# Loading every sixth K tile of an attention kernel by three transfers, of 112, 8 and 8 partitions

## The chip, the cores and the metric

The kernel runs on one core of a Trainium2 chip. The metric is the device time of one execution in microseconds (us). Kernels that were timed ran in alternating rounds with the kernel before, on the same chip. A run more than 1.5% above the fastest of its kernel is called slow, the others fast. The kernel before takes 861.65 us (median of the first 3 runs, 858.39 to 861.66; with two more it is 859.63 us below). In the profiles PE is TensorE, DVE is VectorE, ACT is ScalarE, POOL is GpSimd and SP is SyncE, which issues the transfers; PEld is the loading of weights into TensorE.

## The reference

Two attention blocks whose outputs are concatenated. Block A has 4 K/V heads for 32 query heads; block B, which the change touches, has 32 K/V heads.

```python
def _B_ref(x, k_cache, v_cache, wq, wo):
    B, Sq, D = x.shape                     # 16, 32, 1024
    H, Dh = 32, 128                        # k_cache, v_cache: (16, 32, 1024, 128) bf16
    q = (x @ wq).reshape(B, Sq, H, Dh).transpose(0, 2, 1, 3)
    scores = jnp.einsum("bhqd,bhkd->bhqk", q, k_cache) * (Dh ** -0.5)
    p = _softmax(scores, axis=-1)
    o = jnp.einsum("bhqk,bhkd->bhqd", p, v_cache)
    return o.transpose(0, 2, 1, 3).reshape(B, Sq, H * Dh) @ wo
```

B alone reads 128 MiB of K and as much of V, once each.

## The kernel before

The kernel lists its operations with their buffers, orders them with a scheduler of its own, and works out the semaphore waits. All transfers are issued from SP. A step of B takes four heads of one batch entry: a K tile of 1 MiB and a V tile of 1 MiB.

```python
KB_sb = sb("KB_sb", [P, NKB, 2, 16 * Dh], BF)      # NKB = 2 K tiles of B, 8192 B per partition each
VB_sb = sb("VB_sb", [P, NVB, 4, NCH, Dh], BF)      # NVB = 3 V tiles of B
# ... cut ...
def st_dmaK(q):
    # ... A's K tile cut ...
    sl = q.krslot
    ksrc = pb["k"][q.b, q.h0:q.h0 + 4].rearrange("a (p s) d -> (a p) (s d)", s=32)
    pr.add("sp", lambda e: e.dma_start(KB_sb[:, sl, :, :].rearrange("p i n -> p (i n)"), ksrc),
           writes=[("KB", sl)], dma_key=f"kb{sl}", name="kb_dma", dur=4 * Sk * Dh * 2, wtag={("KB", sl): q.kid})

def st_dmaV(q):
    # ... A's V tile cut; B's: two transfers of two heads each, pieces of 2048 B
    vsrc = pb["v"][q.b, q.h0 + 2 * t_:q.h0 + 2 * t_ + 2].rearrange("a (p c) d -> p a c d", c=NCH)
    # ...
```

A row of the K tile, one partition's share, is 8192 contiguous bytes. VectorE transposes the tile (two instructions of 1.23 us), which frees the buffer for the next load.

Of the kernel before, what the change touches and what calls it, by code (L numbers as in the profile page):

```python
# [12 lines left out]

RINV_LOW, RINV_HIGH = 1e-10, 1e10
NVB_SLOTS = 3
NKB_SLOTS = 2
LAZY_PER_STEP = 100
LAZY_DELAY = 0
# [40 lines left out]
class Prog:  # L59
# [8 lines left out]
        self.specs = []  # L68
        self.vtag = {}

    def add(self, eng, emit, reads=(), writes=(), dma_key=None, name="", dur=None, tag=None, prio=0, wtag=None, rtag=None):
        if rtag:
            for r_, v_ in rtag.items():
                have = self.vtag.get(r_, None)
                assert have == v_, "version mismatch on %r: op %s expects %r but buffer holds %r" % (r_, name, v_, have)
        if wtag:
            for r_, v_ in wtag.items():
                self.vtag[r_] = v_
        if dur is None:
            dur = DUR.get(name, 0.2)  # L80
        self.specs.append((eng, emit, tuple(reads), tuple(writes), dma_key, name, dur, tag, prio))
        op = _Op(eng, emit, name, dur, tag)
        op.prio = prio
        op.idx = len(self.ops)
        deps = {}
        for r in reads:
            w = self.last_w.get(r)
            if w is not None and w is not op:
                deps[w] = 1
        for w_ in writes:  # L90
            lw = self.last_w.get(w_)
            if lw is not None and lw is not op:
                deps[lw] = 1
            for rd in self.readers.get(w_, ()):
                if rd is not op:
                    deps[rd] = 1
        for r in reads:
            self.readers.setdefault(r, []).append(op)
        for w_ in writes:
            self.last_w[w_] = op  # L100
            self.readers[w_] = []
        op.deps = list(deps.keys())
        if dma_key is not None:
            op.dma_key = dma_key
            self.dma_count[dma_key] = self.dma_count.get(dma_key, 0) + 1
            op.dma_val = 16 * self.dma_count[dma_key]
        self.ops.append(op)
        return op
# [91 lines left out]
    def list_schedule(self, lat=0.2, dma_bw=DMA_BW, dma_lat=1.8, look=0.1):  # L200
        ops = self.ops
        n = len(ops)
        users = [[] for _ in range(n)]
        ndeps = [0] * n
        for op in ops:
            ndeps[op.idx] = len(op.deps)
            for d in op.deps:
                users[d.idx].append(op.idx)

        def odur(op):  # L210
            if op.dma_key is not None:
                return 0.06 + op.dur / dma_bw + dma_lat
            return op.dur
        bl = [0.0] * n
        for i in range(n - 1, -1, -1):
            m = 0.0
            for u in users[i]:
                v = bl[u] + lat
                if v > m:
                    m = v  # L220
            bl[i] = odur(ops[i]) + m + ops[i].prio + PRIO_BONUS.get(ops[i].name.split("@")[0], 0.0)
        ready_t = [0.0] * n
        free = {}
        ready = {}
        for i in range(n):
            if ndeps[i] == 0:
                ready.setdefault(ops[i].eng, []).append(i)
        order = []
        pe_mode = [0]
        sp_order = [i for i in range(n) if ops[i].eng == "sp"]  # L230
        sp_pos = [0]
        dma_free = [0.0]

        def sw(i):
            if ops[i].eng != "pe":
                return 0.0
            return MODE_SWITCH if PE_MODE.get(ops[i].name, 0) != pe_mode[0] else 0.0
        while True:
            best = None
            bkey = None  # L240
            for eng, lst in ready.items():
                if not lst:
                    continue
                fe = free.get(eng, 0.0)
                if eng == "sp":
                    fe = max(fe, dma_free[0] - SP_AHEAD)
                if eng == "sp" and SP_STRICT:
                    ci = sp_order[sp_pos[0]]
                    if ci not in lst:
                        continue  # L250
                    st = max(ready_t[ci], fe)
                    key = (st, -bl[ci])
                    if bkey is None or key < bkey:
                        bkey = key
                        best = ci
                    continue
                emin = min(max(ready_t[i], fe) + sw(i) for i in lst)
                cand = [i for i in lst if max(ready_t[i], fe) + sw(i) <= emin + look]
                ci = max(cand, key=lambda i: (bl[i] - 8.0 * sw(i), -i))
                st = max(ready_t[ci], fe) + sw(ci)  # L260
                key = (st, -bl[ci])
                if bkey is None or key < bkey:
                    bkey = key
                    best = ci
            if best is None:
                break
            op = ops[best]
            ready[op.eng].remove(best)
            if op.eng == "sp":
                sp_pos[0] += 1  # L270
            st = max(ready_t[best], free.get(op.eng, 0.0)) + sw(best)
            if op.eng == "sp":
                st = max(st, dma_free[0] - SP_AHEAD)
            if op.eng == "pe":
                pe_mode[0] = PE_MODE.get(op.name, 0)
            op.t0 = st
            if op.dma_key is not None:
                free[op.eng] = st + 0.06
                xs = max(st + 0.06, dma_free[0])
                dma_free[0] = xs + op.dur / dma_bw  # L280
                op.t1 = dma_free[0] + dma_lat
            else:
                op.t1 = st + op.dur
                free[op.eng] = op.t1
            order.append(best)
            for u in users[best]:
                uo = ops[u]
                same_pe = (op.dma_key is None and op.eng == uo.eng and uo.eng == "pe")
                r = op.t1 + (0.0 if same_pe else lat)
                if uo.dma_key is not None:  # L290
                    r += DMA_MARGIN.get(uo.name, DMA_MARGIN_DEFAULT)
                if r > ready_t[u]:
                    ready_t[u] = r
                ndeps[u] -= 1
                if ndeps[u] == 0:
                    ready.setdefault(uo.eng, []).append(u)
        assert len(order) == n, "cycle in dependency graph?"
        seq = sorted(range(n), key=lambda k: (ops[order[k]].t0, k))
        newp = Prog()
        for k in seq:  # L300
            eng, emit, reads, writes, dma_key, name, dur, tag, prio = self.specs[order[k]]
            newp.add(eng, emit, reads, writes, dma_key, name, dur, tag, prio)
        return newp

    def report(self, a, b, engs=("pe", "act", "dve", "sp")):
# [21 lines left out]
    def run_engine(self, eng_name, eng, sems):  # L327
        for op in self.ops:
            if op.eng != eng_name:
                continue  # L330
            for key, val in op.waits:
                eng.wait_ge(sems[key[1]], val)
            last = op.emit(eng)
            if op.dma_key is not None:
                last.then_inc(sems[op.dma_key], 16)
            elif op.sig is not None:
                last.then_inc(sems[op.eng], 1)

# [143 lines left out]
def build(nc, pa, pb, out):  # L482
    P = 128
# [5 lines left out]
    Dh = pa["k"].shape[3]  # L489
    Sk = pa["k"].shape[2]  # L490
# [26 lines left out]
    pr = Prog()  # L517
    with contextlib.ExitStack() as stack:
# [24 lines left out]
        KB_sb = sb("KB_sb", [P, NKB, 2, 16 * Dh], BF)  # L543
# [231 lines left out]
        def st_dmaK(q):  # L775
            if q.pi == 0:
                if not q.kv_new:
                    return
                sl = q.kvslot
                pr.add("sp", lambda e: e.dma_start(KA_sb[:, sl, :, :], pa["k"][q.b, q.s].rearrange("(p c) d -> p c d", c=NCH)),  # L780
                       writes=[("KA", sl)], dma_key=f"ka{sl}", name="ka_dma", dur=Sk * Dh * 2, wtag={("KA", sl): q.kid})
            else:
                sl = q.krslot
                ksrc = pb["k"][q.b, q.h0:q.h0 + 4].rearrange("a (p s) d -> (a p) (s d)", s=32)
                pr.add("sp", lambda e: e.dma_start(KB_sb[:, sl, :, :].rearrange("p i n -> p (i n)"), ksrc), writes=[("KB", sl)], dma_key=f"kb{sl}", name="kb_dma", dur=4 * Sk * Dh * 2, wtag={("KB", sl): q.kid})

        def st_dmaV(q):
            if q.pi == 0:
# [367 lines left out]
```

## Time and profile before

| | before |
|---|---|
| time | 861.65 us |
| DMA rate over the profiled span | 398 GB/s |
| PE, DVE, ACT busy | 84%, 63%, 52% |
| chain of waits, share of DMA | 53%, of which K tiles of B 40% |
| 8192 B packets: median | 309 ns |

The chain of waits is the work that ended last, followed back from the last instruction. A packet is one piece that a DMA engine moves: for a K tile, one row: the page counts 16507 packets of 8 KB or more (135547 less 119040), 16384 rows of 128 tiles and 123 of instructions.

The page of the kernel before, cut to its lines on DMA: the busy share of the DMA engines in 40 slices of the span (9 is 90% or more), the rate in each slice, the packets and the queue that carries the loads.

```profile
DMA  9999999999999999999999999999999999999994
GB/s 341 366 400 412 413 412 389 413 415 399 413 400 385 413 410 412 402 400 411 403 412 404 406 411 401 411 408 408 413 403 412 412 409 412 414 411 409 411 384 174
DMA packets 135547, 341.57 MB, mean 398 GB/s; under 512 B 10496, under 2 KB 26880, under 8 KB 119040
...
q1 hardware_dynamic: 135424, 339.78, 101.1%
```

The engines are busy from start to end at a rate that hardly varies. The packets are the other half of the reading: the trace records each one, and an 8192 B packet takes 309 ns, 26.5 GB/s on one engine; sixteen such engines give 424 GB/s. So the engines run as fast as their packets let them.

The same kernel in stretches of 8 us, from the table by stage (start and end, length, busy times of the engines with instruction counts, clock, DMA share, GB/s):

```profile
170.00:178.00 8.00, 7.82 (x141) 4.44 (x140) 6.16 (x13) 3.71 (x9) 1.04 (x1) 1.00 1.03 411
178.00:186.00 8.00, 7.60 (x131) 4.21 (x131) 4.74 (x9) 5.42 (x13) 0.24 (x1) 1.00 1.04 412
186.00:194.00 8.00, 6.28 (x106) 4.28 (x107) 4.91 (x12) 5.45 (x12) 0.80 (x1) 1.00 1.03 415
194.00:202.00 8.00, 6.89 (x110) 4.50 (x111) 5.48 (x13) 3.05 (x7) 1.04 (x1) 1.00 1.04 411
```

The last two columns matter: DMA share about 1, rate 411 to 415 GB/s in each of these four.

The longest wait of VectorE (the list of waits: us in total, times, longest), and the transfer of the K tile (count, KB each, median us from issue to landing):

```profile
DVE KBt_sb L820 <- DMA KB_sb<-in_B_k_cache_dram: 93.9, 82, 3.1
```

```profile
KB_sb<-in_B_k_cache_dram SPq DMA_DIRECT2D x128, 1024.0 KB, 9.1
```

### The profile page before, as it was taken

How to read it: one execution, taken by the hardware profiler on the slowest of the kernel's cores; microseconds unless marked ns; L12 is line 12 of the kernel's file. 1: busy time of each engine (PE TensorE's matmuls, PEld its weight loads, DVE VectorE, ACT ScalarE, POOL GpSimd, SP SyncE). 2: the span in 40 equal slices, each digit the busy share in tenths (PEclk: the TensorE clock that was granted, in tenths of full speed). 3: DMA queues.
4: the chain of work that ended last, by engine and by line, in shares of the span. 5: the costliest groups of instructions: out<-in, count | busy, mean ns of one | idle time of the engine just before them, and what ended most of it. 6: DMA issues, size and time to landing. Idle time of an engine off the chain costs nothing.

```text
span 857.6 us, 27298 instructions
## 1 busy us (share of the span) xinstructions
PE 717.3 (84%) x11970; PEld 436.2 (51%) x12098; DVE 541.5 (63%) x1115; ACT 447.1 (52%) x981; POOL 67.9 (8%) x76
## 2 busy tenths in 40 slices
PE   3999998898978789888897979988889778878885
PEld 2546655455545455555554545545455445545452
DVE  1655566666657477577674756757777656666674
ACT  1456766466544464546554545544565554555452
POOL 0001000100000000000000000000000000000000
PEclk9999999999999999999999989999999999999898
DMA  9999999999999999999999999999999999999994
GB/s 341 366 400 412 413 412 389 413 415 399 413 400 385 413 410 412 402 400 411 403 412 404 406 411 401 411 408 408 413 403 412 412 409 412 414 411 409 411 384 174
DMA packets 135547, 341.57 MB, mean 398 GB/s; under 512 B 10496, under 2 KB 26880, under 8 KB 119040
## 3 DMA queue, kind: packets, MB, share of 16 engines
q1 hardware_dynamic: 135424, 339.78, 101.1%
q8 instruction: 96, 1.57, 0.7%
q14 instruction: 27, 0.22, 0.1%
HBM read 337.64 MB, written 2.10 MB: 396 GB/s over the span
## 4 chain that ended last, share of the span: by engine, by line
DMA 53%; PE 19%; DVE 15%; SPq 6%; issue 4%; ACT 2%; POOL 1%; POOLq 0%; DVEq 0%
DMA KB_sb<-in_B_k_cache_dram 40%; DVE KBt_sb L820 12%; DMA VA_sb<-in_A_v_cache_dram 5%; PE ps_pj L709 4%; PE ps_s L855 3%; DMA woA_sb<-in_A_wo_dram 3%; PE ps_pj L651 3%; PE ps_pj L668 2%; SPq L800 2%; PE ps_o L947 2%; PE ps_kt L913 2%; SPq L682 1%; PE ps_s L838 1%; PE ps_pt L897 1%; DMA woB_sb<-in_B_wo_dram 1%
## 5 line engine op out<-in xcount | busy, mean ns | idle before, releaser
L820 DVE STREAM_TRANSPOSE KBt_sb<-KB_sb 128x1024 f32<-128x1024 f32 x256 | 306.1, 1226 | 97.7 <-DMA KB_sb<-in_B_k_cache_dram 93.9
L878 ACT ACTIVATE P_sb<-ps_s 128x512 bf16<-128x512 f32 x256 | 152.4, 600 | 84.1 <-PE ps_s L855 74.5
L870 ACT ACTIVATE PTA_sb<-ps_s 128x1024 bf16<-128x1024 f32 x128 | 131.3, 1026 | 104.2 <-PE ps_s L838 91.5
L855 PE MATMUL ps_s<-KBt_sb,QB_sb 32*32 32x512 bf16 x4096 | 146.9, 395 | 10.1 <-DVE KBt_sb L820 5.5
L582 ACT COPY PT_sb<-ps_pt 128x512 f32<-128x512 f32 x128 | 74.9, 585 | 105.7 <-PE ps_o L947 88.6
L794 POOL COPY VAp_sb<-VA_sb 128x1024 bf16<-128x1024 bf16 x64 | 66.6, 1041 | 761.9 <-DMA VA_sb<-in_A_v_cache_dram 729.4
L897 PE MATMUL ps_pt<-id,P_sb 128*128 128x128 f32 x512 | 105.5, 305 | 9.3 <-ACT P_sb L878 7.3
L947 PE MATMUL ps_o<-VB_sb,PT_sb 128*32 128x128 bf16 x4096 | 81.6, 221 | 23.7 <-DMA VB_sb<-in_B_v_cache_dram 16.6
L897 PEld LDWEIGHTS ps_pt<-id,P_sb 128*128 128x128 f32 x512 | 82.7, 206 | 35.2 <-ACT P_sb L878 17.7
L947 PEld LDWEIGHTS ps_o<-VB_sb,PT_sb 128*32 128x32 bf16 x4096 | 60.0, 97 | 60.2 <-issue 56.9
L913 PE MATMUL ps_kt<-VAp_sb,PTA_sb 128*128 128x129 bf16 x1024 | 80.8, 222 | 10.9 <-POOL VAp_sb L794 4.9
L913 PEld LDWEIGHTS ps_kt<-VAp_sb,PTA_sb 128*128 128x128 bf16 x1024 | 67.5, 99 | 36.5 <-POOL VAp_sb L794 14.9
L838 PE MATMUL ps_s<-QT_sb,KTA_sb 128*128 128x256 bf16 x512 | 82.2, 275 | 3.0 <-DVE KTA_sb L584 2.0
L855 PEld LDWEIGHTS ps_s<-KBt_sb,QB_sb 32*32 32x32 bf16 x4096 | 49.3, 90 | 60.9 <-DVE KBt_sb L820 10.6
L709 PE MATMUL ps_pj<-woA_sb,OTA_sb 128*128 128x512 bf16 x224 | 64.0, 394 | 17.4 <-DMA woA_sb<-in_A_wo_dram 10.0
L963 DVE TENSOR_SCALAR OB_sb<-ps_o,rinv_all 128x128 bf16<-128x128 f32 x128 | 43.7, 342 | 53.4 <-PE ps_o L947 52.6
L709 PE MATMUL ps_pj<-woB_sb,OTB_sb 128*128 128x512 bf16 x206 | 62.0, 394 | 16.6 <-ACT OTB_sb L582 4.5
L668 PE MATMUL ps_pj<-xT_sb,wq_sb 128*128 128x512 bf16 x234 | 64.2, 389 | 8.4 <-DMA wq_sb<-in_B_wq_dram 3.4
L651 PE MATMUL ps_pj<-xT_sb,wq_sb 128*128 128x512 bf16 x232 | 63.9, 380 | 8.3 <-DMA wq_sb<-in_A_wq_dram 4.1
L883 DVE TENSOR_TENSOR stat<-stat 64x1 f32<-64x1 f32 x256 | 41.9, 164 | 32.0 <-ACT P_sb L878 24.4
L838 PEld LDWEIGHTS ps_s<-QT_sb,KTA_sb 128*128 128x128 bf16 x512 | 45.0, 98 | 25.5 <-issue 4.4
L722 DVE TENSOR_TENSOR acc<-acc,ps_pj 128x512 f32<-128x512 f32 x64 | 43.0, 672 | 20.1 <-PE ps_pj L709 19.7
(49 smaller groups left out, 533.0 us busy)
## 6 DMA issues: line engine op xcount, KB each, us to landing
KB_sb<-in_B_k_cache_dram SPq DMA_DIRECT2D x128, 1024.0 KB, 9.1
VB_sb<-in_B_v_cache_dram SPq DMA_DIRECT2D x256, 512.0 KB, 9.8
KA_sb<-in_A_k_cache_dram SPq DMA_DIRECT2D x64, 256.0 KB, 10.3
VA_sb<-in_A_v_cache_dram SPq DMA_DIRECT2D x64, 256.0 KB, 9.6
wq_sb<-in_B_wq_dram SPq DMA_DIRECT2D x32, 256.0 KB, 8.6
wq_sb<-in_A_wq_dram SPq DMA_DIRECT2D x32, 256.0 KB, 8.5
woB_sb<-in_B_wo_dram SPq DMA_DIRECT2D x32, 256.0 KB, 10.8
woA_sb<-in_A_wo_dram SPq DMA_DIRECT2D x32, 256.0 KB, 10.1
```

The costliest lines, as they stand in the source:

```text
L582: pr.add("act", lambda e: e.copy(dst_ap, src_ap), reads=reads, writes=writes, name=name + "@act", wtag=wtag, rtag=rtag)
L651: last = e.matmul(ps_pj[:, 0:tn], wq_sb[:, 0, j, hc * Dh:(hc + 1) * Dh], xT_sb[:, 0, j, t0:t0 + tn], start=(j == 0), stop=(j == DJ - 1))
L668: last = e.matmul(ps_pj[:, 0:NTOK], w, xT_sb[:, 1, j, :], start=(j == 0), stop=(j == DJ - 1))
L709: last = e.matmul(ps_pj[:, 0:OUTW], OT[:, gp, hh, :], wo_[:, hh, oh * OUTW:(oh + 1) * OUTW], start=(hh == 0), stop=(hh == nh - 1))
L820: pr.add("dve", lambda e: e.transpose(KBt_sb[:, sl, t_, :].bitcast(F32).rearrange("p (s r i) -> p s r i", r=2, i=32), KB_sb[:, rs, t_, :]. ...
L838: last = e.matmul(ps_s[:, sbf, c2, i * 2 * P:(i + 1) * 2 * P], KTA_sb[:, sl, c * P:(c + 1) * P], qt, start=True, stop=True)
L855: last = e.matmul(ps_s[32 * cg:32 * cg + 32, sbf, g, :].rearrange("p (sh cl j) -> p sh cl j", sh=4, cl=4), lhsT, kt[32 * a:32 * a + 32, g, ...
L870: pr.add("act", lambda e: e.activation(dst, src, ACTF.Exp, scale=scale), writes=BK_S[sbf] + [("PTA", q.half)], name="expA", rtag={("Sv", s ...
L878: pr.add("act", lambda e, src=src, dst=dst, g=g: e.activation(dst, src, ACTF.Exp, scale=scale, accum_out=st[:, g:g + 1]), writes=[BK_S[sbf ...
L897: last = e.transpose(ps_pt32[:, m * P:(m + 1) * P], p32[:, m:Sk // 2:NPK], id32[:])
L913: last = e.matmul(ps_kt[:, qh * OA0:qh * OA0 + Dh + 1], PTA_sb[:, h, c, qh * P:(qh + 1) * P], VAp_sb[:, sl, 4 * h + c, 0:Dh + 1], start=(h ...
L947: last = e.matmul(ps_o[32 * a:32 * a + 32, 0:Dh], PT_pairs[:, c // 2, 32 * (a ^ (c // 4 * 2)):32 * (a ^ (c // 4 * 2)) + 32, c % 2], VB_sb[ ...
```

## The change

Every sixth K tile of B, 21 of 128, is cut into rows 0 to 111, 112 to 119 and 120 to 127. The intent, as the name in the code (LOW_EVERY) suggests, is to move load onto some of the DMA engines: if a transfer of 8 partitions is spread over 8 engines only, and both small transfers over the same 8, those carry 9 rows of the tile and the others 7. The rest of the diff lets an operation hold several transfers that count on one semaphore.

```diff
+LOW_EVERY = 6
@@ Prog.add, run_engine and the scheduler (cut): an operation has n_dma transfers
-            self.dma_count[dma_key] = self.dma_count.get(dma_key, 0) + 1
+            self.dma_count[dma_key] = self.dma_count.get(dma_key, 0) + n_dma
...
-                last.then_inc(sems[op.dma_key], 16)
+                for one in last if isinstance(last, list) else [last]:
+                    one.then_inc(sems[op.dma_key], 16)
@@ st_dmaK
-                pr.add("sp", lambda e: e.dma_start(KB_sb[:, sl, :, :].rearrange("p i n -> p (i n)"), ksrc), ...
+                kdst = KB_sb[:, sl, :, :].rearrange("p i n -> p (i n)")
+                cuts = [(0, P - 16), (P - 16, P - 8), (P - 8, P)] if q.t % LOW_EVERY == LOW_EVERY - 1 else [(0, P)]
+                pr.add("sp", lambda e: [e.dma_start(kdst[a:b], ksrc[a:b]) for a, b in cuts], ...
```

More of the change, by code (lines that the diff above doesn't have):

```diff
@@ L69, in __init__, with add @@
         self.vtag = {}
-    def add(self, eng, emit, reads=(), writes=(), dma_key=None, name="", dur=None, tag=None, prio=0, wtag=None, rtag=None):
+    def add(self, eng, emit, reads=(), writes=(), dma_key=None, name="", dur=None, tag=None, prio=0, wtag=None, rtag=None, n_dma=1):
         if rtag:
@@ L80, in add @@
             dur = DUR.get(name, 0.2)
-        self.specs.append((eng, emit, tuple(reads), tuple(writes), dma_key, name, dur, tag, prio))
+        self.specs.append((eng, emit, tuple(reads), tuple(writes), dma_key, name, dur, tag, prio, n_dma))
         op = _Op(eng, emit, name, dur, tag)
@@ L300, in list_schedule @@
         for k in seq:
-            eng, emit, reads, writes, dma_key, name, dur, tag, prio = self.specs[order[k]]
-            newp.add(eng, emit, reads, writes, dma_key, name, dur, tag, prio)
+            eng, emit, reads, writes, dma_key, name, dur, tag, prio, n_dma = self.specs[order[k]]
+            newp.add(eng, emit, reads, writes, dma_key, name, dur, tag, prio, n_dma=n_dma)
         return newp
@@ L784, in st_dmaK @@
                 ksrc = pb["k"][q.b, q.h0:q.h0 + 4].rearrange("a (p s) d -> (a p) (s d)", s=32)
-                pr.add("sp", lambda e: e.dma_start(KB_sb[:, sl, :, :].rearrange("p i n -> p (i n)"), ksrc), writes=[("KB", sl)], dma_key=f"kb{sl}", name="kb_dma", dur=4 * Sk * Dh * 2, wtag={("KB", sl): q.kid})
+                kdst = KB_sb[:, sl, :, :].rearrange("p i n -> p (i n)")
+                cuts = [(0, P - 16), (P - 16, P - 8), (P - 8, P)] if q.t % LOW_EVERY == LOW_EVERY - 1 else [(0, P)]
+                pr.add("sp", lambda e: [e.dma_start(kdst[a:b], ksrc[a:b]) for a, b in cuts], writes=[("KB", sl)], dma_key=f"kb{sl}", name="kb_dma",
+                       dur=4 * Sk * Dh * 2, wtag={("KB", sl): q.kid}, n_dma=len(cuts))
         def st_dmaV(q):
```

## The prediction

> **What bounds the kernel.** The DMA engines. The page shows mean DMA busy "9" in 39 of 40 slices, 398 GB/s over the span, and the hardware queue alone takes 101.1% of 16 engines' span; PE is at 84%, DVE 63%, ACT 52%. The chain of waits is 53% DMA, 40% of it the load of the K tile of B. In the trace's packet records an 8192 B packet takes 309 ns and the next one starts about 306 ns after it, so a balanced K tile (8 rows on each of 16 engines) occupies an engine for about 2.45 us. The count of packets in flight is 16 or, beside an instruction fetch, 15 nearly all the time: no engine has slack. The landings of one transfer on its 16 engines are spread over about 2.5 us, over 4 us at the end, where 7 or 8 engines are early and 8 late.
>
> **What the change does.** 21 of the 128 K tiles (every sixth) change. Bytes and schedule stay. 42 more issues of about 0.45 us on SP, some 19 us, are off the critical path: SP issues 656 in 862 us and waits for buffers for most of the rest.
>
> [...]
>
> 1. Load alone:[...] 21 x 0.306 = 6.4 us (0.75%)[...].
> [...]
>
> The base is saturated, so nearly all of either is on the critical path. [...]
>
> **Prediction: 890 us, 858 to 945. Faster by over 2%: 0.02; within 2%: 0.45; slower by over 2%: 0.53.**
>
> **What would show it.** DMA rate falls from 398 GB/s to about 385; median packet of 8 KB stays 309 ns, but some 300 to 2,000 of them take 0.6 to 1.5 us[...]. With load alone: no longer packets[...]. DVE waits for K tiles, 93.9 us now, grow by about what the kernel loses.
>
> [...]

Passages are cut, and marked. The sum itself was this. By the estimate from the trace, a K tile of 128 rows takes an engine 8 x 0.306 = 2.45 us. A changed tile was put at 7 x 0.306 = 2.1 us for the 112 rows and 2 x 1.22 us for the two small transfers, 4.6 us together: 2.1 us more, 21 times, 45 us. The 1.22 us, four times the 0.306 us of the trace, was an assumption. One row more on some of the engines, the 6.4 us, was the smaller alternative; "either" is these two. The 45 us were discounted to 30, hence 890 us. The 309 and 306 ns, the packets in flight and the landings are from the trace of the kernel before, where each of the 656 transfers has 16 landing packets (10496); the 0.45 us of an issue is an estimate from the issues there (medians of 0.34 to 0.47 us for the K and V loads). Cut too: 858 to 868 us if the larger term came to nothing, and over 945 us if the 112 rows cost something themselves.

## The result

| | before | after |
|---|---|---|
| time, median of 5 | 859.63 us (858.39 to 861.66) | 950.69 us (942.17 to 952.69) |
| ratio | | 1.104 (95% interval 1.100 to 1.109) |
| profiled span | 857.6 us | 940.3 us |
| DMA rate | 398 GB/s | 363 GB/s |
| 8192 B packets that took over 386 ns (a quarter above 309) | 242 | 2851 |
| 2048 B packets that took over 105 ns (a quarter above 84) | 484 | 7486 |

A ratio is the mean time of one kernel's fast runs over that of the other's fast runs of the same rounds, so not quite the ratio of the medians quoted. Where a difference in us is given below for a timed run, it is (ratio - 1) times the median before of the same rounds: here 0.104 x 859.6 = 90 us slower.

The page of the kernel after:

```profile
DMA  9999999999999999999999999999999999999994
GB/s 336 375 370 400 331 361 369 350 413 341 393 360 412 351 381 373 360 374 339 378 353 391 364 412 345 336 411 354 407 324 359 408 338 406 330 397 350 390 325 163
DMA packets 135887, 341.61 MB, mean 363 GB/s; under 512 B 10833, under 2 KB 27217, under 8 KB 119377
...
q1 hardware_dynamic: 135760, 339.78, 100.3%
```

The engines are as busy as before (100.3% against 101.1%), with the same bytes, at a lower rate. This is a busy share that hides a slowdown: the packets themselves take longer. Slices near 412 GB/s stand beside slices of 324 to 341.

The packets under 512 B grew from 10496 to 10833. They are taken to be the packets that report the landing of a share: 10496 is 16 for each of the 656 transfers. Then 42 small transfers with 8 shares each make 336 of the 337 more. So each small transfer ran in 8 shares, and the 112-row transfers kept their 16. That 8 shares are 8 of the 16 engines agrees with the DMA share of 0.48 at which 8-row loads alone ran (below).

The stretches around one changed tile, whose three transfers are issued together from 177.35 us (the timeline of SP):

```profile
177.35 1.14 SPq L789 DMA_DIRECT2D KB_sb<-in_B_k_cache_dram  x3
```

```profile
170.00:178.00 8.00, 5.29 (x104) 2.72 (x90) 6.02 (x8) 4.30 (x9) 1.04 (x1) 1.00 1.02 400
178.00:186.00 8.00, 7.83 (x98) 5.10 (x96) 5.25 (x10) 4.58 (x11) 1.04 (x1) 1.00 1.00 259
186.00:194.00 8.00, 5.36 (x90) 3.00 (x87) 4.28 (x10) 3.22 (x7) 0.00 (x0) 1.00 1.03 385
194.00:202.00 8.00, 7.02 (x129) 3.83 (x127) 5.75 (x10) 5.35 (x11) 1.04 (x1) 1.00 1.05 420
```

In the 8 us after the issue the rate is 259 GB/s at a DMA share of 1.00; two stretches later it is back at 420. Each changed tile makes such a burst: by the packet records, each of the 21 is followed within 16 us by a stretch of 8 us at 217 to 320 GB/s. From 412 to 259 GB/s for 8 us is a loss of (412 - 259) x 8 / 412 = 3.0 us, and 1.3 us more are lost on average in its flanks and elsewhere (90 / 21 = 4.3 us per changed tile).

The packet records close the account. Summed over all packets, the time above the medians grew by 707 engine-us for the 8192 B packets, 490 for the 2048 B packets, which the change does not touch, and 19 for the 1024 B ones. That is 1216 / 16 = 76 us per engine, of the 82.7 us by which the profiled spans differ.

```profile
DVE KBt_sb L825 <- DMA KB_sb<-in_B_k_cache_dram: 138.4, 74, 6.4
```

```profile
KB_sb<-in_B_k_cache_dram SPq DMA_DIRECT2D x107, 1024.0 KB, 10.8
KB_sb<-in_B_k_cache_dram SPq DMA_DIRECT2D x21, 896.0 KB
...
KB_sb<-in_B_k_cache_dram SPq DMA_DIRECT2D x42, 64.0 KB
```

VectorE's wait for K tiles grew by 44.5 us only. Other waits on landed data grew too: that of POOL for V tiles of A from 729.4 to 820.2 us, that of PE for V tiles of B from 16.6 to 34.3 us.

### The profile page after: what moved, and what is told of

Same layout as the page of the kernel before. It is cut to its first block, busy times and chain, and to the rows that moved or that the text cites. A ratio compares the mean times of both kernels' runs of the same rounds, so it can differ in the third digit from the quotient of the medians.

```text
span 940.3 us, 27468 instructions
## 1 busy us (share of the span) xinstructions
PE 758.5 (81%) x12098; PEld 447.9 (48%) x12098; DVE 544.2 (58%) x1115; ACT 448.8 (48%) x981; POOL 67.9 (7%) x76
## 3 DMA queue, kind: packets, MB, share of 16 engines
q1 hardware_dynamic: 135760, 339.78, 100.3%
## 4 chain that ended last, share of the span: by engine, by line
DMA 51%; PE 25%; DVE 12%; SPq 6%; issue 3%; ACT 1%; POOL 1%; POOLq 0%; DVEq 0%
DMA KB_sb<-in_B_k_cache_dram 33%; DVE KBt_sb L825 9%; DMA VB_sb<-in_B_v_cache_dram 7%; DMA VA_sb<-in_A_v_cache_dram 6%; PE ps_pj L711 5%; PE ps_s L860 5%; DMA woA_sb<-in_A_wo_dram 3%; PE ps_pj L670 3%; PE ps_o L952 2%; PE ps_pj L653 2%; PE ps_kt L918 2%; PE ps_pt L902 2%; SPq L789 2%; PE ps_s L843 2%; PE ps_kt L816 1%
## 5 line engine op out<-in xcount | busy, mean ns | idle before, releaser
L860 PE MATMUL ps_s<-KBt_sb,QB_sb 32*32 32x512 bf16 x4096 | 153.0, 409 | 11.5 <-DVE KBt_sb L825 5.8
L799 POOL COPY VAp_sb<-VA_sb 128x1024 bf16<-128x1024 bf16 x64 | 66.6, 1041 | 844.2 <-DMA VA_sb<-in_A_v_cache_dram 820.2
L952 PE MATMUL ps_o<-VB_sb,PT_sb 128*32 128x128 bf16 x4096 | 84.9, 227 | 48.3 <-DMA VB_sb<-in_B_v_cache_dram 34.3
L902 PE MATMUL ps_pt<-id,P_sb 128*128 128x128 f32 x512 | 108.0, 311 | 9.7 <-ACT P_sb L883 7.7
L952 PEld LDWEIGHTS ps_o<-VB_sb,PT_sb 128*32 128x32 bf16 x4096 | 62.9, 100 | 86.6 <-issue 83.2
L918 PE MATMUL ps_kt<-VAp_sb,PTA_sb 128*128 128x129 bf16 x1024 | 83.7, 227 | 17.5 <-POOL VAp_sb L799 13.2
L918 PEld LDWEIGHTS ps_kt<-VAp_sb,PTA_sb 128*128 128x128 bf16 x1024 | 70.0, 101 | 44.4 <-POOL VAp_sb L799 21.9
L711 PE MATMUL ps_pj<-woB_sb,OTB_sb 128*128 128x512 bf16 x256 | 77.5, 414 | 11.6 <-DMA woB_sb<-in_B_wo_dram 5.4
L711 PE MATMUL ps_pj<-woA_sb,OTA_sb 128*128 128x512 bf16 x256 | 71.6, 396 | 15.6 <-DMA woA_sb<-in_A_wo_dram 11.8
L860 PEld LDWEIGHTS ps_s<-KBt_sb,QB_sb 32*32 32x32 bf16 x4096 | 49.6, 92 | 66.8 <-issue 16.6
L670 PE MATMUL ps_pj<-xT_sb,wq_sb 128*128 128x512 bf16 x256 | 69.8, 394 | 7.8 <-DMA wq_sb<-in_B_wq_dram 5.4
L653 PE MATMUL ps_pj<-xT_sb,wq_sb 128*128 128x512 bf16 x256 | 69.5, 383 | 6.2 <-DMA wq_sb<-in_A_wq_dram 3.0
```

What stands on the lines that cost most here:

```text
L653: last = e.matmul(ps_pj[:, 0:tn], wq_sb[:, 0, j, hc * Dh:(hc + 1) * Dh], xT_sb[:, 0, j, t0:t0 + tn], start=(j == 0), stop=(j == DJ - 1))
L670: last = e.matmul(ps_pj[:, 0:NTOK], w, xT_sb[:, 1, j, :], start=(j == 0), stop=(j == DJ - 1))
L711: last = e.matmul(ps_pj[:, 0:OUTW], OT[:, gp, hh, :], wo_[:, hh, oh * OUTW:(oh + 1) * OUTW], start=(hh == 0), stop=(hh == nh - 1))
L860: last = e.matmul(ps_s[32 * cg:32 * cg + 32, sbf, g, :].rearrange("p (sh cl j) -> p sh cl j", sh=4, cl=4), lhsT, kt[32 * a:32 * a + 32, g, ...
L902: last = e.transpose(ps_pt32[:, m * P:(m + 1) * P], p32[:, m:Sk // 2:NPK], id32[:])
L918: last = e.matmul(ps_kt[:, qh * OA0:qh * OA0 + Dh + 1], PTA_sb[:, h, c, qh * P:(qh + 1) * P], VAp_sb[:, sl, 4 * h + c, 0:Dh + 1], start=(h ...
```

## The experiments

Three theories stood at the start. A: the two 8-row transfers cost (the larger term of the prediction's sum). B: the 112-row transfer costs by itself. C: three transfers in place of one, or transfers of fewer than 128 partitions, cost as such. All edits are of the changed kernel; `cuts` and `parts` are what a changed tile loads. The sets of runs were made on different chips, so differences between sets are differences of their ratios, good to about 6 us (the intervals are given).

### The 112 rows alone

```diff
-cuts = [(0, P - 16), (P - 16, P - 8), (P - 8, P)] if ...
+cuts = [(0, P - 16)] if ...
```

Rows 112 to 127 then hold older data. The result is wrong by construction; the comparison with the reference did not notice, so its tolerance says nothing here.

> The 112-row transfer of every sixth K tile alone, without the two of 8 rows (rows 112 to 127 keep older data: the result is wrong on purpose). Theory A, my prediction's term: the cost lies in the 8-row transfers[...]. Then this kernel is 21 x 0.306 = 6 us faster than before (one row less per engine), 848 to 858 us. Theory B: the cost lies in the 7-row shares of the 112-row transfer[...]. Then most of the 90 us stays: 900 to 940 us. Theory C, three transfers in place of one cost something as such: as A, about 853 us.

Measured: 923.93 us (913.57 to 930.85; one run, the profiled one, slow: it is in the median and not in the ratio), ratio 1.069 (1.061 to 1.076), 59 us slower than before while loading less. Theory A falls as the main cause, and B is supported. The two small transfers add the remaining 90 - 59 = 31 us, give or take 8. The other packets suffer here too: 6906 of the 2048 B packets took over 105 ns, against 7486 with the small transfers (in a slow run, but before has 484).

### Three transfers by columns

```diff
+parts = [(kdst[:, a:b], ksrc[:, a:b]) for a, b in ((0, 3584), (3584, 3840), (3840, 4096))]
```

> Every sixth K tile by three transfers of all 128 partitions, split by columns (7168, 512 and 512 B of each row). Same number of transfers, same bytes[...]. Theory C (three transfers cost as such, by issue, completion or shorter rows): well above 880 us. Theories A and B[...]: within 5 us of before[...].

Measured: 861.21 us, ratio 0.999 (0.997 to 1.001). The number of transfers costs nothing that can be seen, so the first half of theory C falls.

### 112 and 16 rows

```diff
+cuts = [(0, P - 16), (P - 16, P)] if ...
```

> 112 rows and one transfer of 16 rows: all 16 engines then carry 8 rows, so nothing is uneven. If the uneven load[...] mattered much, this is much faster than the change (below 900 us). [...] Theory B: near the change, 920 to 950 us.

Measured: 939.97 us (933.00 to 945.62), ratio 1.089 (1.083 to 1.094), 76 us slower than before. If both transfers are spread evenly over the 16 engines, as the DMA shares of 0.97 and 0.99 of such loads alone (below) suggest, every engine carries 8 rows here, and most of the loss is still there. Uneven load is then at most a small part of it.

### Two halves

```diff
+cuts = [(0, P // 2), (P // 2, P)] if ...
```

> Every sixth K tile in two halves of 64 partitions: even load on 16 engines, no small transfer. [...] a tile costs an engine 4.9 us in place of 2.45: 21 x 2.45 = 51 us, 890 to 930 us. [...]

Measured: 942.86 us, ratio 1.095 (1.090 to 1.101), 82 us slower: above the 51 us worked out, and above the range given. The 4.9 us of that sum, twice the 2.45 us of a whole tile, was the author's assumption; no trace of before shows a factor of two. Of the 8192 B packets 2274 took 450 to 700 ns (82 in the kernel before), around twice 309 ns.

### Small transfers, the same source rows, three kinds of place

The control loads the left half of each changed tile only. The other three add four 8-row loads of 4096 B rows into the free right half, all from source rows 112 to 119; only the destination partitions differ. All four are wrong on purpose, which the comparison again did not notice. "Own", "foreign" and "four" are labels and no more. The 0.153 us of a 4096 B row in the expectations is an estimate, half the 0.306 us of 8192 B.

```diff
+parts = [(kdst[:, 0:2048], ksrc[:, 0:2048])]                                                # control
+      + [(kdst[r, 2048:4096], ksrc[P - 16:P - 8, 2048:4096]) for r in ROWS]
+# own:     0:32:4   32:64:4   1:32:4   33:64:4     (start:stop:step)
+# foreign: 64:96:4  96:128:4  65:96:4  97:128:4
+# four:    80:88    88:96     112:120  120:128
```

> Control for the next three. Every sixth K tile loads only the left half of each row (128 partitions of 4096 B; the right half keeps older data, wrong on purpose). 0.5 MB less, 21 times: 21 x 8 x 0.153 = 26 us less than before, about 834 us, by every theory.

> The control and four 8-row transfers of 4096 B rows, all from the same source rows, into partitions 0, 4 .. 28, then 32, 36 .. 60, then the same plus 1[...]. Load theory: 21 x 4 x 0.153 = 13 us over the control[...]. [...] Theory that small 8-partition transfers are slow as such (or that reading the same source is): as slow as the next two.

> As the run before, same sizes, same source rows, but into partitions 64, 68 .. 92 and so on[...]. [...] Load theory and any theory of the source side: equal to the run before within 3 us.

> As the two runs before, but into partitions 80 to 87, 88 to 95, 112 to 119, 120 to 127[...], as the small transfers of the change. [...] Load theory: equal to the two before.

| | median | ratio to before | over the control |
|---|---|---|---|
| control | 842.26 us | 0.979 (0.976 to 0.983) | |
| own | 851.20 us | 0.990 (0.985 to 0.996) | 0.0111 x 861 = 9.6 us |
| foreign | 868.49 us | 1.009 (1.006 to 1.012) | 25.4 us |
| four | 868.74 us | 1.009 (1.006 to 1.011) | 25.2 us |

The control saved 18 us, not 26; why is open. Between "own" and "foreign" nothing differs but the partitions they land in, and the cost goes from 9.6 to 25.4 us, with intervals that stay apart. The ordinary traffic shows it as well: 603, 837, 3871 and 4093 of the 2048 B packets took over 105 ns in control, own, foreign and four. That rules out the source side and the size of a transfer for these loads. "Own" costs 9.6 us where the added load alone was put at 12.9, equal within the noise. "Foreign" had been put at 20 to 35 us and "four" at 35 to 60, and "four" missed its range: eight partitions in a row cost no more here than eight that lie 4 apart from 64 on. Packets of about four times the usual length, which the prediction's second term assumed, hardly occur. In "four" 10 of the 4096 B packets took 0.55 us or more (4 x 0.153 = 0.61), against 7 in the control; in the kernel after, 38 of the 8192 B packets took 1 us or more, against 31 before. Why is open.

### The transfers alone

A kernel that computes nothing and issues eight K loads at a time, for nine sets of rows, waiting between them. Its output is wrong.

```diff
+PHASES = [slice(0, 128), slice(0, 112), slice(0, 96), slice(0, 64), slice(64, 128), slice(112, 128),
+          slice(112, 120), slice(0, 32, 4), slice(64, 96, 4)]
```

> The transfers by themselves, nothing computed, the output wrong on purpose: nine stretches of eight back-to-back K loads of 8192 B rows, each stretch waited for, into partitions 0-127, 0-111, 0-95, 0-63, 64-127, 112-127, 112-119, then eight rows 4 apart from 0 and eight rows 4 apart from 64. [...] 0-127 about 420 GB/s with packets of 309 ns;[...] both stretches of rows 4 apart: packets of 309 ns, held back only by the issue of about 0.45 us each. Theory of uneven load or of the source side: packets of about 309 ns in all of them.

The table by stage, one line for each set of rows in this order (start and end, length, POOL's busy time, clock, DMA share, GB/s):

```profile
1.70:22.50 20.80, 0.00 (x0) 1.00 1.00 403
24.10:51.80 27.70, 0.00 (x0) 1.00 0.97 264
53.20:78.80 25.60, 0.00 (x0) 1.00 0.98 246
80.80:101.10 20.30, 0.00 (x0) 1.00 0.98 205
103.10:123.50 20.40, 0.00 (x0) 1.00 0.99 205
125.70:134.50 8.80, 0.00 (x0) 1.00 0.99 119
136.80:145.70 8.90, 0.00 (x0) 1.00 0.48 60
148.40:153.80 5.40, 0.00 (x0) 1.00 0.33 96
155.60:161.00 5.40, 0.00 (x0) 1.00 0.32 94
```

The first six lines have the DMA engines equally busy (0.97 to 1.00), at 403, 264, 246, 205, 205 and 119 GB/s. Eight loads of 112 rows take 27.7 us where eight of 128 rows take 20.8: fewer bytes, more time. The median packet is 309 ns for 128 rows, 496 for 112, 636 and 639 for the halves, 1202 for rows 112 to 127 and 1198 for rows 112 to 119. The last two lines, eight partitions 4 apart, are bound by the issue: SP starts one every 0.67 us. Their packets, forecast at 309 ns, had medians of 456 and 419 ns; this miss is not explained, so only packets from a full queue are compared. In the lines of rows 112 to 127 and 112 to 119, with nothing else in the queue, a packet does take the 1.2 us of the prediction's second term, and in the halves about twice 309 ns.

### Every twelfth tile

```diff
-LOW_EVERY = 6
+LOW_EVERY = 12
```

> The change at every twelfth K tile (10 tiles in place of 21). If each changed tile costs for itself, as a burst of 8 to 10 us that ends before the next: 10/21 of 90 us, about 43 us more than before, 900 to 908 us. If the lasting unevenness of the load mattered[...]: much less than half, below 885 us.

Measured: 903.15 us (897.07 to 908.65), ratio 1.050 (1.047 to 1.054), 43 us, which is 4.3 us for each of the 10 tiles, as for each of the 21. The loss is a sum of separate bursts.

### Mixed and spaced transfers alone

> Transfers by themselves again, 16 in each stretch, output wrong on purpose. (1) 16 x 128 rows: 39 us at 2.45 us each. (2) 16 x 112 rows: 53 us, at the 3.3 us each that the run before showed. (3) 128 and 112 rows in turn: 46 us if each keeps its own time; more, up to 63 us (8 x 2.45 + 8 x (2.14 + 3.3), the extra 3.3 us that a changed tile's 112 rows cost in the kernel)[...]. (4) 14 x 128 and 2 x 112: 41 against 45 us. (5) 16 x 64 rows: 39 us. (6) 128 and 64 in turn: 39 us additive, 45 us if ordinary traffic is held up. (7) 64 source rows in a row into every second partition[...]: faster than (5)[...], about 20 to 35 us; equal to (5) if the source or the number of rows limits. (8) 128 and 8 rows in turn. (9) Eight partitions 112 to 119 from source rows 4 apart:[...] about 1.1 us each, 18 us, packets near 1.2 us; (10) eight partitions 4 apart from source rows 112 to 119: about 0.5 us each, bound by the issue, 8 to 10 us, packets below 0.6 us. If the source rows matter and not the partitions, (9) and (10) change places.

```diff
+# shortened
+PHASES = [128], [112], [128, 112 in turn], [4 x 128, 112, 3 x 128], [0:64], [128, 0:64 in turn],
+         [0:128:2 from source rows 0:64], [128, 112:120 in turn], [112:120 from 0:32:4], [0:32:4 from 112:120]
```

Ten stretches of 16 loads; the lines of the 1st to 5th, the 7th, the 9th and the 10th, as in the last table:

```profile
1.70:42.50 40.80, 0.00 (x0) 1.00 1.00 411
44.00:92.80 48.80, 0.00 (x0) 1.00 1.00 301
94.50:139.80 45.30, 0.00 (x0) 1.00 1.00 347
141.60:185.40 43.80, 0.00 (x0) 1.00 0.99 377
187.30:228.00 40.70, 0.00 (x0) 1.00 1.00 206
...
274.70:296.80 22.10, 0.00 (x0) 1.00 0.94 380
...
331.60:350.30 18.70, 0.00 (x0) 1.00 0.48 54
352.80:363.40 10.60, 0.00 (x0) 1.00 0.32 96
```

Sixty-four source rows into every second partition run at 380 GB/s, with median packets of 309 ns, where the same rows into partitions 0 to 63 run at 206 with 639 ns. The last two lines swap source and destination of an 8-row load: the slow one is the one whose destination is partitions 112 to 119, whatever it reads. So the partitions decide, not the source and not the number of rows. The third line is near what the first two give by addition (20.4 + 24.4 = 44.8 us), so an alternating stream does not multiply the loss. The fourth does not add up so well: two loads of 112 rows among sixteen should give 41.8 us and took 43.8, so each costs 1.5 us here, against 0.5 us in the second line (which missed its 53 us). What such a load costs depends on what runs beside it. The 6th stretch (42.6 us, 40.8 by addition) lies between its two forecasts; the 8th (31.2 us) had none.

### Even and odd partitions in the kernel

This is the test of what is left of theory C, and the sharpest one: two transfers of 64 rows, as in the halves, but interleaved.

```diff
+parts = [(kdst[j:P:2], ksrc[j:P:2]) for j in range(2)]
```

> Every sixth K tile in two transfers of 64 rows each, as in the run with halves (82 us slower than before), but of the even and of the odd partitions instead of the lower and the upper half. Same bytes, same number of transfers, same rows per engine[...]. [...] within 8 us of before, 855 to 868 us. [...] If fewer than 128 partitions cost as such: as the halves, 935 to 950 us.

The first range is for the case that these partitions do as well here as alone, where the packets took 309 ns.

Measured: 860.51 us (858.02 to 863.11), ratio 1.001 (0.998 to 1.004), correct. The page of this kernel, to be compared with those of before and after (first the rate of the run with halves, then this one):

```profile
GB/s 339 373 329 411 332 370 355 358 410 340 388 341 406 354 398 360 379 367 349 366 320 401 330 414 332 355 384 351 413 343 363 405 336 412 343 405 338 412 328 180
```

```profile
GB/s 333 383 397 411 413 411 386 413 415 400 415 401 395 412 411 413 401 400 410 411 413 403 397 413 413 405 407 411 415 398 412 413 408 412 413 412 410 410 379 189
DMA packets 135884, 341.58 MB, mean 399 GB/s; under 512 B 10832, under 2 KB 27216, under 8 KB 119376
```

The dips are gone, and 225 of the 8192 B packets took over 386 ns, as few as before. Same bytes, rows and number of transfers as in the halves, which cost 82 us: which partitions a transfer reaches is the whole difference. (Rows per engine are taken to be the same too: alone, both kinds of 64 rows kept the DMA engines 0.94 to 1.00 busy.) So it is shown that the partitions decide. Why they do is not shown; no record names the engine of a packet.

### Why it costs more in the kernel than alone

A changed tile costs 2.8 us (112 rows, 59 / 21), 4.3 us (the change) and 3.9 us (halves) in the kernel. The next run issues the stream of K and V loads alone, 24 tiles a stretch, of which two are changed.

```diff
+# shortened
+PHASES = [128], [112], [112, 8, 8], [0:64, 64:128], [0:128:2, 1:128:2]     # what tiles 6 and 14 load
```

> The kernel's stream of K and V loads alone, nothing consumed, 24 tiles a stretch (12 K of 8192 B rows, 12 V of 2048 B pieces), output wrong on purpose. (1) all of 128 rows: 12 x 2.45 + 12 x 2.56 = 60 us and about 1.5 us of start. Then two of the K tiles changed: (2) 112 rows only, (3) 112, 8 and 8 as in the change, (4) halves, (5) even and odd partitions. If the cost is all in the DMA engines[...], each changed tile costs here what it costs in the kernel: (2) 2 x 3.0 = 6 us more than (1), (3) 8.6 us, (4) 7.8 us, (5) under 1 us. If the waits for buffers in the kernel make it larger: clearly less than that in (2) to (4), about half.

```profile
1.80:65.20 63.40, 0.00 (x0) 1.00 1.01 396
66.70:132.40 65.70, 0.00 (x0) 1.00 1.01 379
133.90:203.10 69.20, 0.00 (x0) 1.00 1.02 364
204.60:272.70 68.10, 0.00 (x0) 1.00 1.02 370
274.30:338.00 63.70, 0.00 (x0) 1.00 1.01 395
```

Per changed tile, half the difference to the first line: 1.15, 2.9, 2.35 and 0.15 us. The order is that of the kernel, the sizes are 40 to 70% of it, between the two forecasts. In this stream the landings of one transfer on its 16 engines are spread over 0.8 us (median of all transfers), in the kernel before over 2.5 us. So the last run is meant to hold some engines back, by small loads of 8, 4 and 2 rows into partitions 4 apart after the second tile; the expectation for a larger spread is the one that doubles the cost of a tile.

```diff
+SKEW = (0, 32, 4), (32, 64, 4), (1, 32, 4), (2, 16, 4), (34, 48, 4), (3, 16, 4), (35, 40, 4), (33, 40, 4)
+for rows in SKEW: (one 8192 B row load each, into a slot of its own)
```

> The stream of K and V loads as in the run before, but after the second tile of each stretch[...] the landings of one transfer spread over about 2.5 us as they do in the kernel, in place of 0.8. [...] a changed tile costs about twice what it cost in step, (2) 2.5 to 3.3 us in place of 1.15, (3) 4 us in place of 2.9, (4) 3.5 to 4 us in place of 2.35, (5) still under 0.5. If the remainder comes from the kernel's waits for buffers: the same as in step, within 0.5 us.

```profile
1.70:69.20 67.50, 0.00 (x0) 1.00 0.98 378
70.80:145.80 75.00, 0.00 (x0) 1.00 0.94 336
147.40:223.90 76.50, 0.00 (x0) 1.00 0.98 333
225.50:300.90 75.40, 0.00 (x0) 1.00 0.99 338
302.40:367.60 65.20, 0.00 (x0) 1.00 1.00 391
```

Per changed tile 3.75, 4.5 and 3.95 us, close to the kernel's 2.8, 4.3 and 3.9 and well above those in step; the first missed its range upwards. This supports the spread of the engines as the reason, since nothing is consumed here and no buffer is waited for. A measure that does not hang on the length of the first stretch says the same: the time of the packets above the medians 309 and 84 ns, per changed tile and engine, is 1.3, 3.0 and 2.5 us in step and 2.6, 4.4 and 4.5 us here. It does not settle it: the run is a single look, and the spread differs from stretch to stretch. Before the first changed tile the landings were 3.2 us apart at most in (2) and 1.5 us in (4). In (2) they drifted to 6.9 us, so a part of its 3.75 us is engines that end late. The fifth stretch did not get the spread at all (landings within 0.9 us), so its line cannot be compared with the first.

## Why the prediction was wrong

- **What bounds the kernel: right.** DMA share stayed at 100%, and 76 of the 82.7 us are longer packets.
- **How the small transfers are spread: right in number.** 8 landing packets per small transfer (336 of the 337 more); which engines carry them is not shown.
- **Load alone, 6.4 us: minor, as said.** With even load (112 and 16 rows) 76 of the 90 us remained.
- **The step that failed: the first term of the sum, 7 x 0.306.** That the small transfers cost more than their load was right. But the prediction put a changed tile at 7 x 0.306 + 2 x 1.22 = 4.6 us, not 2.45. The first term, 2.1 us, takes a row of the 112-row transfer to be as quick as a row of a whole tile, which makes it 21 x 0.306 = 6.4 us cheaper than before over the kernel. Measured, 112 rows alone are 59 us dearer than before: the term is off by 65 us, and comes to 2.45 + 59 / 21 = 5.3 us per tile. Alone, 112 rows run at 264 or 301 GB/s in place of 403 or 411. The prediction named a cost of the 112 rows themselves as a risk (over 945 us) and left it out of the sum.
- **The second term was too large.** 2 x 1.22 x 21 = 51 us were given for the 8-row transfers, on an assumed factor of four; they added about 31. The two errors partly cancel: 65 us too little, 20 too much, 45 in all. Packets of 1.2 us occur when such transfers run alone, and hardly in the kernel (38 against 31 at 1 us or more).
- **The discount went the wrong way.** 45% were given to a change within 2%, and the estimate of 45 us was discounted to 30, although the prediction itself had said that no engine had slack. The measured loss is 90 us.
- **Signs.** The rate was to fall to about 385 GB/s and fell to 363; the median packet stayed at 309 ns; 1015 of the 8192 B packets took 0.6 to 1.5 us (144 before), in the range of 300 to 2,000 given. This hit is luck: it was forecast for the 8-row transfers, and the run without them (profiled in its slow run) has 1010. Not foreseen: 2048 B packets of tiles that were not changed carry 490 of the 1216 engine-us. DVE's wait for K tiles was to grow by about the loss and grew by half of it.

The intent found no room in this kernel either: the engines were at 101.1% before the change and at 100.3% after it, so none is seen to have slack that moved load could use. No version faster than the kernel before came out of the runs; the interleaved pair equals it.

## What to carry to other kernels

When the DMA engines are saturated, the set of partitions that a transfer reaches can matter more than its size or number: in this kernel, cutting 21 of 128 tiles by columns (ratio 0.999) or into interleaved partitions (1.001) cost nothing, cutting them into contiguous runs of partitions 9 to 10% (1.089 to 1.104). A busy share of DMA that stayed at 100% while the rate fell from 398 to 363 GB/s came from longer packets here (2851 of 8192 B over 386 ns, against 242), so look at the durations of the packets, including those of transfers that you did not touch. When a sum has one term per transfer, price the large one by its own shape too, before the odd small ones.
